# Cosine attention and a leaky-ReLU block on one core: norms issued 12 steps sooner in the visits, one remainder tile moved to a visit's end

## The chip, the cores and the metric

The kernel runs on 1 core of one Trainium2 chip. The metric is device time in microseconds (us): the median of the runs of one program. A profiled execution gives the trace; its span runs from the first to the last instruction, and its own device time lies a little above the span.

## The reference

Cosine attention over 8 batches, 12 heads, 448 tokens and head size 64, then two dense layers with a leaky ReLU between them:

```python
q_n = q / (norm(q) + 1e-06); k_n = k / (norm(k) + 1e-06)
scores = q_n @ k_n.T / tau
attn = exp(scores - max) / sum
x = (attn @ v), heads side by side        # 3584 x 768
h = x @ w_in                              # 768 x 2048
out = maximum(0.01 * h, h) @ w_out        # 2048 x 768
```

## The kernel before

**Tiles.** Two heads make a pair, called a slot `s` in the code: 6 slots in a batch, 48 in all. The 448 tokens of a head are 3 blocks of 128 (block `ki` = 0, 1, 2) and a remainder of 64. A *key tile* `(s, ki)` is the scores of one key block of a slot against all 448 queries, for both heads: two matmuls on TensorE (L259) into a pair of PSUM banks, and one exponential on ScalarE (L271) that reads the pair. The remainders of two slots together make one *remainder tile*, written `(s, 3)` with odd `s`: four matmuls that read the transposed queries and keys of slots `s - 1` and `s`, and again one exponential.

**A norm** of slot `s` (`norm`, L637) is a chain over five queues. `sums` (L178) are two VectorE reductions of squares that GpSimd made before (L167). `roots` are two ScalarE activations (L185, L186). `normalise` is four VectorE instructions (L197, L198, L202 twice) that write `qn`. `transposes` is a transposing DMA on SyncE's queue (L234) that turns `qn` into `qkT`, the operand of the key tiles. Then come the four loads of a later slot (`load_qk`, SyncE's queue), a one-element copy on GpSimd that waits for `qn` (`hold`, L478), and the squares of slot `s + 1` on GpSimd. So the squares of one slot start when the slot before it is normalised.

**The order of work.** The schedule is written by hand: each engine takes its instructions in the order in which the program issues them, and an instruction that waits holds all behind it on its engine or queue. Batches 3 to 7 each have a *visit* (the loop at L691). With `s0 = 6 * b`, a visit is:

1. `attend` for groups of four heads of the batch before: totals and products on TensorE (L282), reciprocal totals on ScalarE (L293, L294), scaling on VectorE (L313). Batch 3 has one of these here, the others three.
2. Loads of V on GpSimd's queue (L146, L154).
3. Two remainder tiles, `(s0 + 1, 3)` and `(s0 + 3, 3)` (L700).
4. *Tokens*: blocks of 128 output rows of an earlier chunk of the second dense layer (`both_halves`, L392). A token is 32 steps of two matmuls (L412) that gather in one pair of banks, kept for the whole token. Between the steps, by the table `after`, the 18 key tiles of the batch are issued. There are 3 tokens in the visits of batches 3, 4 and 6 (tiles after steps 5, 11, 16, 16, 21 and 27 of each) and 4 in those of 5 and 7. At the token's end VectorE copies the rows out (L421) and SyncE's queue stores them (L388).
5. The last remainder tile, `(s0 + 5, 3)` (L714).
6. `first`: 16 groups of the first dense layer (six matmuls L336 and one ScalarE activation L343 each).

**Banks.** `banks` deals the pair that was dealt longest ago among those not kept; a token keeps one of the four pairs, so the key tiles turn over in the other three.

**Norms inside a visit, before.** At the top of token `i` (`i` = 0, 1, 2) `sums(s0 + 4 + i)`; after step 16 of that token, behind its two tiles there, `norm(s0 + 4 + i)`. During `first`: sums of `s0 + 7`, `s0 + 8`, `s0 + 9` at `m` = 0, 5, 10 and their norms at `m` = 2, 7, 12. So in a visit of 3 tokens the tiles of slot `s0 + 5` begin at step 16 of token 2, one token after the step at which its norm is issued. Slot `s0 + 3` of batch 3, slot 21, is normalised in the last unit ahead of that visit (L662, L663, L674).

Of the kernel before, what the change touches and what calls it, by code (L numbers as in the profile page):

```python
# [16 lines left out]
def kernel(  # L17
# [61 lines left out]
    def banks(count, keep=None, which=None):  # L79
        lo, hi = (0, 8) if not deals["apart"] else (0, 4) if count == 2 else (4, 8)  # L80
        x = which if which is not None else min(
            (i for i in range(lo, hi, count) if not set(range(i, i + count)) & set(sum(kept.values(), []))),
            key=lambda i: max(age[i : i + count]),
        )
        deals["n"] += 1
        age[x : x + count] = [deals["n"]] * count
        if keep:
            kept[keep] = list(range(x, x + count))
        return ps[:, x] if count == 1 else ps[:, x : x + count]

    def given_back(keep):
        deals["n"] += 1
        for i in kept.pop(keep):
            age[i] = deals["n"]
# [63 lines left out]
    def squares(s, engs=(gp, gp)):  # L158
        if s >= NSLOT:
            return  # L160
        tiles = []
        for x, eng, name in zip(raw[s], engs, ("sq0", "sq1")):
            sq = sqp.tile(list(x.shape), F32, name=name)
            if eng is nc.scalar:
                nc.scalar.activation(sq, x, func=AF.Square)
            else:
                eng.tensor_tensor(sq, x, x, op=ALU.mult)  # L167
            tiles.append(sq)
        sqs[s] = tiles

    def sums(s, parts=(0, 1)):
        if s >= NSLOT:
            return
        if s not in ss:
            ss[s] = smp.tile([128, 14], F32, name="ss")
        for i in parts:
            o = ss[s][:, 0:8] if i == 0 else ss[s][:, 8:14]
            nc.vector.tensor_reduce(  # L178
                o.rearrange("p (h t) -> p h t", h=2), sqs[s][i], axis=AX.X, op=ALU.add
            )  # L180

    def roots(s):
        if s >= NSLOT:
            return
        nc.scalar.activation(ss[s], ss[s], func=AF.Ln, bias=tiny)  # L185
        nc.scalar.activation(ss[s], ss[s], func=AF.Exp, scale=0.5)  # L186
        if s < 2:
            nc.scalar.activation(ss[s], ss[s], func=AF.Identity, bias=eps)
# [3 lines left out]
    def normalise(s):  # L192
        if s >= NSLOT:
            return
        r = smp.tile([128, 14], F32, name="r")
        if s >= 2:
            nc.vector.tensor_scalar_add(ss[s], ss[s], 1e-6)  # L197
        nc.vector.reciprocal(r, ss[s])  # L198
        qn[s] = qnp.tile([128, 7, 2, D], BF16, name="qn")
        for x, lo, hi, r0 in ((raw[s][0], 0, 4, 0), (raw[s][1], 4, 7, 8)):  # L200
            nt = hi - lo
            nc.vector.tensor_tensor(  # L202
                qn[s][:, lo:hi],
                x.rearrange("p h t d -> p t h d"),
                r[:, r0 : r0 + 2 * nt].rearrange("p (h t) -> p t h", h=2)
                .unsqueeze(3).to_broadcast([128, nt, 2, D]),
                op=ALU.mult,
            )
# [19 lines left out]
    def transposes(s):  # L228
        if s >= NSLOT:
            return  # L230
        dst = qtp.tile([128, 7, 128], BF16, name="qkT")
        qkT[s] = dst.rearrange("p t c -> p (t c)")
        if s >= DMA_FROM:
            nc.sync.dma_start(  # L234
                out=dst, in_=qn[s].rearrange("p t h d -> p (t h d)"), transpose=True
            )
            return
        tp = transposed()
        one(tp, s, 0, 7)
        nc.vector.tensor_copy(out=dst, in_=tp)  # L240
# [6 lines left out]
    def key_tiles(which):  # L247

        tiles = []
        for s, ki in which:  # L250
            sc = banks(2)
            tiles.append(sc)
            for i in range(2 if ki == 3 else 1):
                x = qkT[s - 1 + i] if ki == 3 else qkT[s]
                for a in range(2):
                    rows = slice(64 * a, 64 * a + 64)
                    out = sc[64 * i : 64 * i + 64] if ki == 3 else sc
                    c0, c1 = (448, 512) if ki == 3 else (512 + 128 * ki, 640 + 128 * ki)
                    nc.tensor.matmul(  # L259
                        out=out[:, a, :S], lhsT=x[rows, c0:c1], rhs=x[rows, 0:S],  # L260
                        start=True, stop=True,
                    )
        for (s, ki), sc in zip(which, tiles):
            if ki == 3:
                pr[s // 2] = prp.tile([128, 2, S], BF16, name="pr")
                dst = pr[s // 2]
            else:
                if s not in pe:
                    pe[s] = pep.tile([128, 3, 2, S], BF16, name="pe")
                dst = pe[s][:, ki]  # L270
            nc.scalar.activation(out=dst, in_=sc[:, :, :S], func=AF.Exp, scale=inv_tau)  # L271
# [50 lines left out]
    def chunk_cols(c):  # L322
        return (0, MAIN) if c % 2 == 0 else (MAIN, 512)
# [3 lines left out]
    def first(c, m, kts=range(KT)):  # L327

        c0, n = chunk_cols(c)
        if c not in hT:  # L330
            hT[c] = htp.tile([128, MT, 512], BF16, name="hT")
        if (c, m) not in pms:
            pms[c, m] = banks(1)
        pm = pms[c, m]
        for kt in kts:
            nc.tensor.matmul(  # L336
                out=pm[:, :n],
                lhsT=w_in_sb[:, kt, m * 128 : (m + 1) * 128],
                rhs=xT[c // 2][:, kt, c0 : c0 + n],
                start=(kt == 0), stop=(kt == KT - 1),  # L340
            )
        if kts[-1] == KT - 1:
            nc.scalar.activation(  # L343
                out=hT[c][:, m, :n], in_=pms.pop((c, m))[:, :n], func=AF.Prelu, alpha=0.01
            )
            if (c, m, 0) in kept:
                given_back((c, m, 0))
# [79 lines left out]
    for c in range(B):  # L427
        c0, n = chunk_cols(c)
# [47 lines left out]
    def hold(x):  # L476
        seen = smp.tile([128, 1], F32, name="seen")
        gp.tensor_copy(out=seen, in_=x)  # L478
# [27 lines left out]
    for s in range(NPAIR):  # L506
        j = s // 2 - 1 if s >= 2 else None
        even = s % 2 == 0
        n = s + 2 if s + 2 <= NPAIR else None
# [52 lines left out]
    def attend(j):  # L562
        totals(j)
        po = banks(2)
        for e in range(2):
            products(j, e, po[:, e])
        for e in range(2):
            scale(j, e)
# [64 lines left out]
    def load_next(s):  # L633
        for n in (s + 2,) if s <= NPAIR + 6 else (s + 2, s + 3) if s == NPAIR + 7 else (s + 3,):
            load_qk(n)

    def norm(s):  # L637
        if s >= NSLOT:
            return
        roots(s)  # L640
        normalise(s)
        transposes(s)
        load_next(s)
        hold(qn[s][:, 6, 0, 0:1])
        squares(s + 1)
# [45 lines left out]
    for b in range(3, B):  # L691
        for j in range(b * NQ - 1 if b == 3 else (b - 1) * NQ, b * NQ):
            attend(j)
        for j in range(b * NQ, (b + 1) * NQ):
            if j not in vb:
                load_v(j)
        load_v_rem(b + 1)
        s0 = b * NPAIR
        tiles = [(s0 + p, ki) for p in range(NPAIR) for ki in range(3)]
        key_tiles([(s0 + 1, 3), (s0 + 3, 3)])  # L700
        for i, (c, ts) in enumerate(tokens):
            if i < 3:
                sums(s0 + 4 + i)
            if len(tokens) == 3:
                after = {5: 1, 11: 1, 16: 2, 21: 1, 27: 1}
            else:
                after = {8: 1, 16: 2, 21: 1, 27: 1} if i < 2 else {8: 1, 16: 2, 24: 1}
            for n, _ in enumerate(both_halves(c, ts), 1):
                for _ in range(after.get(n, 0)):
                    key_tiles([tiles.pop(0)])  # L710
                if n == 16 and i < 3:
                    norm(s0 + 4 + i)
        assert not tiles
        key_tiles([(s0 + 5, 3)])  # L714
        for m in range(MT):
            if m in (0, 5, 10):
                sums(s0 + 7 + m // 5)
            if m in (2, 7, 12):
                norm(s0 + 7 + m // 5)
            first(b - 1, m)  # L720
        tokens = [(b - 1, ts) for ts in range(chunk_cols(b - 1)[1] // 128)]
    for j in range((B - 1) * NQ, B * NQ):
        attend(j)
# [40 lines left out]
```

## Time and profile before

| what | value |
|---|---|
| runs | 427.1, 427.34, 428.75 us; median 427.34 |
| profiled execution | 429.06 us, its span 427.2 us |
| mean granted TensorE clock | 0.995 |
| busy, share of the span | TensorE 96%, ScalarE 61%, VectorE 46%, GpSimd 32% |

By stage, from the busy time of each engine in stretches of the span (us):

| stretch | what | length | TensorE busy | ScalarE busy |
|---|---|---|---|---|
| 122.0 to 150.4 | end of batch 2, batch 3's attend and tokens | 28.40 | 25.60 | 20.78 |
| 173.0 to 193.7 | batch 4's tokens (3) | 20.70 | 20.11 | 18.50 |
| 221.4 to 246.6 | batch 5's tokens (4) | 25.20 | 25.20 | 18.42 |
| 269.2 to 289.9 | batch 6's tokens (3) | 20.70 | 20.09 | 18.49 |
| 317.7 to 342.8 | batch 7's tokens (4) | 25.10 | 25.10 | 18.07 |

In the profile PE is TensorE's matmuls, PEld its weight loads, ACT ScalarE, DVE VectorE, POOL GpSimd, SP SyncE's queue. A line of a timeline gives the start, the length, engine, source line, operation, tiles and count of the instructions merged into it; in brackets stands the idle time before it and what ended that. PEclk is the granted TensorE clock as a share of full speed.

### The profile page before, as it was taken

To read this page: it belongs to the slowest core of one execution; us is meant where nothing else is said; L and a number is where in the kernel's file an instruction comes from. 1 tells how busy PE (TensorE), PEld (TensorE's weight loads), DVE (VectorE), ACT (ScalarE), POOL (GpSimd) and SP (SyncE) were. 2 spreads that over 40 slices of the span, in tenths; PEclk is the share of its full clock that TensorE was granted. 3 is DMA by queue.
4 is the path that set the end of the run, shared out by engine and by line. 5 is a ranking of instruction groups with operands and counts; after the bars stand their busy time and mean duration, and the time that the engine had idled before them with its cause. 6 is when DMAs were issued, how large, how long until landed. Compare 5 with 4: busy or idle time off the path is not lost.

```text
span 427.2 us, 9731 instructions
## 1 busy us (share of the span) xinstructions
PE 410.6 (96%) x3873; PEld 213.9 (50%) x3873; DVE 197.5 (46%) x412; ACT 262.6 (61%) x448; POOL 136.8 (32%) x208
## 2 busy tenths in 40 slices
PE   8689999999989999999999999999999999999995
PEld 3234455544435555554455555554455555554563
DVE  5785867646562564555444454555444201310021
ACT  3887785678856965885568665885568655114300
POOL 4757523543474235333351315333321000000000
PEclk9999999999998999999999999999999999999999
DMA  7999997997587787586384756576362410010022
GB/s 173 186 245 230 209 221 130 182 202 156 129 130 122 173 187 145 58 176 173 90 124 88 182 144 137 61 174 175 88 78 60 97 38 2 39 75 0 0 75 74
DMA packets 102894, 53.72 MB, mean 126 GB/s; under 512 B 68929, under 2 KB 97857, under 8 KB 102849
## 3 DMA queue, kind: packets, MB, share of 16 engines
q1 hardware_dynamic: 77296, 40.98, 40.2%
q0 software_dynamic: 25056, 11.80, 21.8%
q8 instruction: 30, 0.49, 0.5%
q10 hardware_dynamic: 496, 0.33, 0.2%
q14 instruction: 16, 0.12, 0.1%
HBM read 45.61 MB, written 11.01 MB: 133 GB/s over the span
## 4 chain that ended last, share of the span: by engine, by line
PE 87%; DMA 6%; DVE 3%; SPq 1%; issue 1%; ACT 1%; POOL 0%; POOLq 0%; DVEq 0%
PE ps L336 34%; PE ps L412 20%; PE ps L366 14%; PE ps L282 12%; PE ps L259 7%; DMA qkT<-qn 3%; DMA q_h<-in_q_dram 3%; DVE qn L202 2%; DMA q_h<-in_k_dram 1%; SPq L131 1%; PE ps L216 1%; ACT pe L271 0%; DVE ss L197 0%; DVE qkT L240 0%; DVE xT L313 0%
## 5 line engine op out<-in xcount | busy, mean ns | idle before, releaser
L336 PE MATMUL ps<-xT,w_in_sb 128*128 128x384 bf16 (+1 forms) x768 | 149.2, 353 | 0.9 <-DVE xT L313 0.9
L271 ACT ACTIVATE pe<-ps 128x896 bf16<-128x896 f32 x144 | 125.6, 914 | 28.9 <-PE ps L259 27.8
L343 ACT ACTIVATE hT<-ps 128x384 bf16<-128x384 f32 (+1 forms) x128 | 68.4, 542 | 71.2 <-PE ps L336 70.6
L336 PEld LDWEIGHTS <-w_in_sb 128*128 128x128 bf16 x768 | 73.8, 98 | 71.7 <-issue 5.1
L412 PE MATMUL ps<-w_out_sb,hT 64*128 64x384 bf16 x1088 | 102.6, 326 | 0.0
L412 PEld LDWEIGHTS <-hT 64*128 64x128 bf16 x1088 | 53.0, 95 | 39.5 <-issue 3.2
L178 DVE TENSOR_REDUCE ss<-sq 128x8 f32<-128x512 f32 (+1 forms) x96 | 58.2, 616 | 27.2 <-POOL sq L167 23.6
L478 POOL CAST seen<-qn 128x1 f32<-128x1 bf16 x47 | 8.6, 183 | 168.6 <-DVE qn L202 168.4
L259 PE MATMUL ps<-qkT 64*128 64x448 bf16 (+1 forms) x384 | 53.4, 358 | 7.6 <-DMA qkT<-qn 4.0
L366 PE MATMUL ps<-w_out_sb,hT 128*128 128x384 bf16 x352 | 58.9, 326 | 0.0
L313 DVE TENSOR_TENSOR xT<-ps,rb 128x448 bf16<-128x448 f32 x48 | 27.8, 619 | 49.3 <-ACT rb L294 49.3
L167 POOL TENSOR_TENSOR sq<-q_h 128x512 f32<-128x512 f32 x46 | 47.7, 1037 | 4.4 <-DMA q_h<-in_k_dram 3.6
L366 PEld LDWEIGHTS <-hT 128*128 128x128 bf16 x352 | 33.8, 98 | 24.0 <-issue 2.1
L197 DVE TENSOR_SCALAR ss<-ss 128x14 f32<-128x14 f32 x46 | 9.7, 212 | 73.1 <-ACT ss L186 73.0
L167 POOL TENSOR_TENSOR sq<-k_h 128x384 f32<-128x384 f32 x46 | 37.8, 822 | 0.0
L377 DVE COPY osb<-ps 128x384 f32<-128x384 f32 (+1 forms) x22 | 12.0, 547 | 51.7 <-PE ps L366 51.7
L282 PE MATMUL ps<-pe,v_b 128*32 128x448 bf16 x576 | 35.6, 353 | 0.0
L202 DVE TENSOR_TENSOR qn<-q_h,r 128x512 bf16<-128x512 f32 x48 | 33.5, 699 | 1.9 <-DMA q_h<-in_q_dram 0.3
L259 PEld LDWEIGHTS <-qkT 64*128 64x128 bf16 (+1 forms) x384 | 15.5, 97 | 33.2 <-issue 17.6
L271 ACT ACTIVATE pr<-ps 128x896 bf16<-128x896 f32 x24 | 21.6, 917 | 8.2 <-PE ps L259 8.2
L202 DVE TENSOR_TENSOR qn<-k_h,r 128x384 bf16<-128x384 f32 x48 | 26.5, 552 | 0.0
L293 ACT ACTIVATE rb<-ps 128x448 f32<-128x448 f32 x24 | 13.1, 544 | 19.4 <-PE ps L282 19.4
(43 smaller groups left out, 231.6 us busy)
## 6 DMA issues: line engine op xcount, KB each, us to landing
q_h<-in_q_dram SPq DMA_DIRECT2D x48, 192.0 KB, 3.1
k_h<-in_k_dram SPq DMA_DIRECT2D x47, 192.0 KB, 3.1
out_dram<-osb SPq DMA_DIRECT2D x30, 192.0 KB, 2.7
v_b<-in_v_dram POOLq DMA_DIRECT2D x24, 192.0 KB, 5.1
out_dram<-osb SPq DMA_DIRECT2D x12, 384.0 KB, 2.7
w_in_sb<-in_moe_w_in_dram POOLq DMA_DIRECT2D x4, 768.0 KB, 9.9
w_out_sb<-in_moe_w_out_dram POOLq DMA_DIRECT2D x2, 1536.0 KB, 17.5
q_h<-in_q_dram SPq DMA_DIRECT2D x48, 32.0 KB, 3.2
```

Of the source, the lines that this page charges most:

```text
L167: eng.tensor_tensor(sq, x, x, op=ALU.mult)
L178: nc.vector.tensor_reduce(o.rearrange("p (h t) -> p h t", h=2), sqs[s][i], axis=AX.X, op=ALU.add)
L202: nc.vector.tensor_tensor(qn[s][:, lo:hi], x.rearrange("p h t d -> p t h d"), r[:, r0 : r0 + 2 * nt].rearrange("p (h t) -> p t h", h=2) .u ...
L259: nc.tensor.matmul(out=out[:, a, :S], lhsT=x[rows, c0:c1], rhs=x[rows, 0:S], start=True, stop=True,)
L271: nc.scalar.activation(out=dst, in_=sc[:, :, :S], func=AF.Exp, scale=inv_tau)
L282: nc.tensor.matmul(out=x[32 * g : 32 * g + 32, :S], lhsT=weights(g, ki) if ki < 3 else rem(g), rhs=pe[s][:, ki, a, :] if ki < 3 else pr[j] ...
L293: nc.scalar.activation(rb, sm[:, :S], func=AF.Ln)
L313: nc.vector.tensor_tensor(xT[m][:, 2 * jj + e, half * S : (half + 1) * S], pos.pop((j, e))[:, :S], rbs[j], op=ALU.mult,)
L336: nc.tensor.matmul(out=pm[:, :n], lhsT=w_in_sb[:, kt, m * 128 : (m + 1) * 128], rhs=xT[c // 2][:, kt, c0 : c0 + n], start=(kt == 0), stop= ...
L343: nc.scalar.activation(out=hT[c][:, m, :n], in_=pms.pop((c, m))[:, :n], func=AF.Prelu, alpha=0.01)
L366: nc.tensor.matmul(out=po2[:, :HALF], lhsT=hT[c][:, m, ts * 128 : (ts + 1) * 128], rhs=w_out_sb[:, m, half * HALF : (half + 1) * HALF], st ...
L412: last[half] = nc.tensor.matmul(out=po2[:, half, :HALF], lhsT=hT[c][rows, m, ts * 128 : (ts + 1) * 128], rhs=w_out_sb[rows, m, half * HALF ...
```

## The change

The remainder tile `(s0 + 3, 3)` of batch 3's visit leaves the visit's start and is issued at its end, ahead of `(s0 + 5, 3)`; the other batches keep both at the start. The norm of slot `s0 + 4 + i` is issued after step 4 of token `i`, and so ahead of the token's first tile. The sums of `s0 + 5` and `s0 + 6` are issued after step 26 of tokens 0 and 1, and so ahead of the copy of these tokens' rows on VectorE. The sums of `s0 + 4` are issued at the end of the visit before, behind its last group of `first`, so that the next visit's attend with its scaling follows them on VectorE; batch 3 has no visit before it and issues them after its attend, ahead of token 0, as before. No instruction is added or removed: each engine has the same set, in another order.

```diff
-        key_tiles([(s0 + 1, 3), (s0 + 3, 3)])
+        key_tiles([(s0 + 1, 3), (s0 + 3, 3)][: 1 if b == 3 else 2])
+        if b == 3:
+            sums(s0 + 4)
         for i, (c, ts) in enumerate(tokens):
-            if i < 3:
-                sums(s0 + 4 + i)
...
             for n, _ in enumerate(both_halves(c, ts), 1):
                 for _ in range(after.get(n, 0)):
                     key_tiles([tiles.pop(0)])
-                if n == 16 and i < 3:
+                if n == 4 and i < 3:
                     norm(s0 + 4 + i)
+                if n == 26 and i < 2:
+                    sums(s0 + 5 + i)
         assert not tiles
-        key_tiles([(s0 + 5, 3)])
+        key_tiles([(s0 + 3, 3), (s0 + 5, 3)][0 if b == 3 else 1 :])
         for m in range(MT):
...
             first(b - 1, m)
+        sums(s0 + 10)
         tokens = [(b - 1, ts) for ts in range(chunk_cols(b - 1)[1] // 128)]
```

## Prediction

> **What bounds the kernel now.** I read the page's busy shares first, then the chain that ended last, then TensorE's waits.
>
> ```profile
> PE 410.6 (96%) x3873; PEld 213.9 (50%) x3873; DVE 197.5 (46%) x412; ACT 262.6 (61%) x448; POOL 136.8 (32%) x208
> ```
>
> TensorE is busy for all but 427.2 - 410.6 = 16.6 us. The chain gives PE 87% of the span, so a reordering can gain only where TensorE stands still. TensorE's waits over the whole span (engine and line, what it waited for, us in total, times, longest):
>
> ```profile
> PE ps L259 <- DMA qkT<-qn: 4.0, 4, 2.1
> PE ps L259 <- ACT pe L271: 2.3, 5, 1.1
> ```
>
> The second row falls before 50 us: asked from 50 us on, the waits show only the first. So behind the first batch TensorE is held by four transposing DMAs that land late, and by nothing else. TensorE's timeline places them:
>
> ```profile
> 125.40 0.57 PE L259 MATMUL ps<-qkT 64*64 64x448 bf16 x6
> 128.10 0.38 PE L259 MATMUL ps<-qkT 64*64 64x448 bf16 x2 [2.13 <-DMA qkT<-qn]
> ...
> 145.74 0.35 PE L259 MATMUL ps<-qkT 64*128 64x448 bf16 x2
> 146.76 0.36 PE L259 MATMUL ps<-qkT 64*128 64x448 bf16 x2 [0.66 <-DMA qkT<-qn]
> ...
> 190.08 0.36 PE L259 MATMUL ps<-qkT 64*128 64x448 bf16 x2 [0.59 <-DMA qkT<-qn]
> ...
> 286.30 0.36 PE L259 MATMUL ps<-qkT 64*128 64x448 bf16 x2 [0.61 <-DMA qkT<-qn]
> ```
>
> The first is batch 3's second remainder tile: half of it issues (the last two of the six matmuls), then slot 21's transposed tile is missing. The others are the first tile of slot s0 + 5, in token 2 of the three visits with 3 tokens; those with 4 tokens have no wait. Finally the stretches around the first wait (length, then busy us of PE, PEld, DVE, ACT, POOL with counts, then the granted clock, DMA share, GB/s):
>
> ```profile
> 125.97:128.10 2.13, 0.00 (x1) 0.00 (x2) 1.61 (x3) 0.78 (x1) 2.13 (x4) 1.00 1.01 149
> 128.10:129.00 0.90, 0.90 (x10) 0.51 (x12) 0.00 (x0) 0.48 (x1) 0.90 (x2) 1.00 0.88 237
> 129.00:132.25 3.25, 3.25 (x24) 1.55 (x21) 0.00 (x0) 1.35 (x2) 2.15 (x4) 0.51 1.31 176
> ```
>
> 0.9 us after the gap the granted clock is 0.51 for 3.25 us; the stretches that I read between 134.8 and 358.5 are at 1.00.
>
> **What the change is worth, step by step.**
>
> *The moved remainder tile.* A remainder tile takes 0.38 us, so the two would have ended at 125.40 + 0.76 = 126.16; the row says 128.10 + 0.38 = 128.48. Loss: 2.31 us (the idle time shows 2.13, as the last matmul's drain counts as busy). Token 0 needs only slots 18 and 19, so the wait goes and nothing takes its place there: (21, 3) now stands some 19 us later, and slot 21's DMA had landed at 128.1. Its 0.38 us on TensorE and 0.9 us on ACT are moved, not saved. Gain **2.31 us**.
>
> *The half clock.* From the first L412 to token 1's first tile is 128.41 to 137.24 = 8.83 us in batch 3, and 173.48 to 180.64 = 7.16 us in batch 4 with the same work. The slow clock cost 1.67 us. I take it as an answer to the gap: it is TensorE's longest after the first loads. Bounds: 0 if it has another cause, **1.67** if it goes. I take that for the profiled execution. The runs speak for it too: 427.1 and 427.34 against 428.75, and 429.06 profiled, steps of 1.4 to 2.0 us, as if two of four executions had the slow stretch.
>
> [...]
>
> *Slot s0 + 5's norm.* In token 2 the next tile follows 0.19 us behind the first one of step 16 where nothing waits (134.26 to 134.45 and the like). So the losses are 146.76 - 145.93 = 0.83, 190.08 - 189.33 = 0.75, 286.30 - 285.53 = 0.77. Now follow the chain in batch 4, whose visit start doesn't change. ACT, after the two remainder exponentials, reaches the roots at about 175.0 instead of 178.47; sums of s0 + 4 are long done. Roots to `qn` takes 178.47 to 180.70 = 2.2 us, so `qn` is there at 177.2. Then hold and squares 2.0 us (180.84 to 182.87) and the rest of the reductions 0.6 us (182.87 to 183.45): sums of s0 + 5 at about 179.9. Token 0 ends near 180.0, its copies (1.02 us) at 181.0. Roots of s0 + 5 follow the exponential of step 27, at 180.7, `qn` at 182.95, and the DMA lands 2.9 to 3.3 us later, near 186.0, instead of 190.08; wanted at 189.3. That is 3.3 us to spare for a wait of 0.75. The rows' store and the loads stand ahead of this transpose on SP's queue as before; the copy that the store waits for ends 2 us before `qn`. Even the longest landing of a transpose in this trace, 5.1 us, fits. The four loads behind each transpose go out as much sooner, into a buffer whose last readers (normalise and squares of the slot before) are done by then; the transpose itself writes slot s0's buffer (five are in turn), last read by (s0, 2) at step 16 of token 0. On GpSimd only the squares stand behind the hold. Gain **0.83 + 0.75 + 0.77 = 2.35 us**, bounds 0 and 2.35.
>
> *What the sooner norms put in ACT's way.* The roots (0.46 us net) stand ahead of the token's six exponentials, where before four ran first. Exponentials in a row start every 0.81 to 0.88 us: a token asks ACT for 6 x 0.84 + 0.46 = 5.5 us of its 6.33 (180.64 to 186.97). In batch 4 this makes step 5's exponential 0.46 us later, ending at 176.4; its pair is dealt again to the second tile of step 16 at 176.66. It fits by 0.26 us: nothing lost, 0.2 at worst.
>
> Batch 3's token 0 is the tight one, as its sums are not early:
>
> ```profile
> 126.42 1.34 DVE L178 TENSOR_REDUCE ss<-sq 128x8 f32<-128x512 f32 x2
> ...
> 128.67 2.48 POOL L154 DMA_DIRECT2D v_rem<-in_v_dram  x4
> ...
> 143.74 1.25 SPq L234 DMA_TRANSPOSE qkT<-qn  x1
> ```
>
> Token 0 now starts at 125.8. ACT ends the remainder's exponential at 126.75 and then waits in the roots for these sums until 127.8 (before, the roots came at 135.08). Behind it step 5's exponential runs 128.26 to 129.18, though its matmuls are done by 126.95. The second tile of step 16 wants that pair at 128.90 and starts at 129.23: **0.33 us lost**, bounds 0 and 1.0 (ACT's whole wait). From there ACT wins back 6.33 - 5.5 = 0.8 us a token.
>
> GpSimd delays the next norm: the V loads end at 131.15, so hold and squares of slot 23 run to 133.2, sums to 133.8, copies of token 0's rows to 134.8 (that pair is dealt again at 135.4), roots at 133.8, `qn` at 136.0. The transpose, 143.74 in the row above, is issued at 136.0 and lands near 139.0; wanted at 141.9. At the visit's end both remainder tiles find their pairs free: the exponentials of step 16's second tile and step 21 end at 143.8 and 144.7, the tiles come at 145.0 and 145.4. `first` begins near 145.8 instead of 150.4.
>
> *Visits with 4 tokens; sums of s0 + 10.* Nothing waits there now, and ACT has more room (18.4 of 25.2 us busy). The sums of s0 + 10 stand ahead of the attend's scaling: their squares end at 167.4, the sums at 168.0, the scaling starts at 168.23. Cost 0; without that 0.2 us the scaling slips, which TensorE doesn't wait for within the attends' 6.9 us.
>
> *Sum.* Against the profiled execution: 2.31 + 1.67 + 2.35 - 0.33 = 6.00; 429.06 - 6.00 = 423.06 us. Against the median, taken as a run without the slow stretch: 4.33; 427.34 - 4.33 = 423.01. Both give **423.0 us**.
>
> **Rivals.**
> 1. *All runs had the slow stretch, and it goes* (their spread is noise): 427.34 - 6.00 = 421.3. The first three times speak against it, being 1.4 us apart in two clusters.
> 2. *The half clock is no answer to the gap and stays*: against the profiled execution 429.06 - 4.33 = 424.7. [...]
> 3. *The norms come no sooner than the tiles need* (copies now behind the sums, the store ahead of the transpose): the 2.35 stays lost, 427.34 - 2.31 + 0.33 = 425.4, no change. The slack of 3.3 and 2.9 us speaks against it.
> 4. *Slower: ACT waits in each token's roots for the sums*, which now need the squares of the same token. Roots to the next sums is 2.2 + 2.0 + 0.6 = 4.8 us; batch 3's token 0 has 6.0 with GpSimd's V loads. It costs TensorE only if this loop exceeds the token's 6.33 us; then each token takes as long as the loop. Over the 9 tokens of the short visits it eats the gain at 6.8 us, and at 7.1 us the kernel is 2.4 us slower: 429.8. No row shows a loop so long outside of batch 3's start.
>
> **How the numbers follow.** 0.5% is 2.1 us, about what a measurement of this kernel can tell from no change. Forecast 0.62 (422.4 to 424.2), rival 1 0.15, rival 2 0.10, rival 3 0.07, rival 4 0.06. Faster by over 0.5% (below 425.2): the first three, 0.87, less 0.01 for their edge; same 0.08; slower 0.06. The range runs from rival 1 to rival 2: 421.2 to 424.9.
>
> **What would show it.** No TensorE wait for a transposing DMA after 100 us; granted clock 1.00 from 125 to 146; `first` of batch 3 near 145.8; a short wait of an L259 for ACT near 129; batch 4's and 6's tokens 0.75 us shorter, 5's and 7's unchanged. I am wrong if TensorE waits for L271 by more than 1 us in all, or the clock drops at another place.

## The result and the profile after

| | before | after |
|---|---|---|
| runs, us | 427.1, 427.34, 428.75, 429.42 | 422.4, 422.73, 423.05, 423.24 |
| median, us | 428.04 | 422.89 |
| profiled execution, us (span) | 429.06 (427.2) | 422.73 (420.9) |

The ratio is 0.9876, 95% interval 0.9843 to 0.9909: the changed kernel is 1.2% faster. In a later set it took 422.75 us (median of 6) against 427.27 (median of 17), ratio 0.989, interval 0.987 to 0.991. The forecast was 423.0.

The executions of before fall into two groups, with nothing between 427.35 and 428.38 us; the median depends on how many of each are in it. What divides them is the subject of the third experiment.

TensorE's line of the busy shares and the chain by engine, from the page of the changed kernel:

```profile
PE 408.0 (97%) x3873; PEld 214.9 (51%) x3873; DVE 197.9 (47%) x412; ACT 261.1 (62%) x448; POOL 137.1 (33%) x208
...
PE 87%; DVE 4%; DMA 3%; ACT 3%; issue 1%; SPq 1%; POOL 0%; POOLq 0%; ACTq 0%; DVEq 0%
```

TensorE's busy time fell by 2.6 us with the same instructions, mostly because matmuls at half clock count as busy for longer (twelve of L412 2.13 us in before, from 129.76, and 1.14 to 1.16 at the full clock). Its idle time fell from 16.6 to 12.9 us, and in the chain (the work that ended last, followed back) the DMAs' share from 6% to 3%. Asked for from 60 us on, TensorE's waits have no row left. Its timeline at batch 3's tokens:

```profile
125.29 0.38 PE L259 MATMUL ps<-qkT 64*64 64x448 bf16 x4
125.61 0.99 PE L412 MATMUL ps<-w_out_sb,hT 64*128 64x384 bf16 x10
...
128.60 0.86 PE L259 MATMUL ps<-qkT 64*128 64x448 bf16 x4
129.28 0.99 PE L412 MATMUL ps<-w_out_sb,hT 64*128 64x384 bf16 x10
...
141.57 0.56 PE L259 MATMUL ps<-qkT 64*128 64x448 bf16 x4
...
145.04 0.57 PE L259 MATMUL ps<-qkT 64*64 64x448 bf16 x8
145.54 2.77 PE L336 MATMUL ps<-xT,w_in_sb 128*128 128x384 bf16 x16
```

Token 0 starts 0.32 us behind the first remainder tile (before: 3.0 us). The two tiles of step 16 take 0.86 us in token 0 and 0.56 in token 2: that is the new stall of 0.3 us. In token 2 they now run together, where before the second came 0.83 us late. Both remainder tiles stand at the end (x8), and `first` begins at 145.54 instead of 150.35. The stretch that had half the clock, for the changed kernel (length, busy us of PE, PEld, DVE, ACT, POOL with counts, granted clock, DMA share, GB/s):

```profile
129.00:132.25 3.25, 3.15 (x38) 2.14 (x39) 1.06 (x2) 3.25 (x6) 3.25 (x7) 1.00 1.02 117
```

The clock is 1.00, and 38 matmuls stand where there were 24. ScalarE's timeline shows why the stall comes:

```profile
125.73 0.92 ACT L271 ACTIVATE pr<-ps 128x896 bf16<-128x896 f32 x1 [0.67 <-PE ps L259]
127.69 0.31 ACT L185 ACTIVATE ss<-ss,tiny 128x14 f32<-128x14 f32 x1 [1.04 <-DVE ss L178]
128.03 0.21 ACT L186 ACTIVATE ss<-ss 128x14 f32<-128x14 f32 x1
128.15 4.94 ACT L271 ACTIVATE pe<-ps 128x896 bf16<-128x896 f32 x6
```

It waits 1.04 us in the roots for VectorE's sums, then runs six exponentials without a break; the first of them, whose matmuls end at 126.43 + 0.35 = 126.78, could have started near 126.8.

### The profile page after: what moved, and what is told of

Read it like the earlier page. It is cut to its first block, busy times and chain, and to the rows that moved or that the text cites. A ratio compares the mean times of both kernels' runs of the same rounds, so it can differ in the third digit from the quotient of the medians.

```text
span 420.9 us, 9733 instructions
## 1 busy us (share of the span) xinstructions
PE 408.0 (97%) x3873; PEld 214.9 (51%) x3873; DVE 197.9 (47%) x412; ACT 261.1 (62%) x448; POOL 137.1 (33%) x208
## 4 chain that ended last, share of the span: by engine, by line
PE 87%; DVE 4%; DMA 3%; ACT 3%; issue 1%; SPq 1%; POOL 0%; POOLq 0%; ACTq 0%; DVEq 0%
PE ps L336 34%; PE ps L412 20%; PE ps L366 13%; PE ps L282 12%; PE ps L259 7%; DMA q_h<-in_k_dram 3%; DVE qn L202 2%; ACT pe L271 1%; DVE ss L178 1%; PE ps L216 1%; SPq L131 0%; ACT ss L185 0%; ACT ss L186 0%; DVE r L198 0%; DVE xT L313 0%
## 5 line engine op out<-in xcount | busy, mean ns | idle before, releaser
L271 ACT ACTIVATE pe<-ps 128x896 bf16<-128x896 f32 x144 | 122.9, 919 | 25.1 <-PE ps L259 24.5
L412 PE MATMUL ps<-w_out_sb,hT 64*128 64x384 bf16 x1088 | 101.4, 323 | 0.0
L412 PEld LDWEIGHTS <-hT 64*128 64x128 bf16 x1088 | 53.8, 94 | 37.5 <-issue 1.6
L259 PE MATMUL ps<-qkT 64*128 64x448 bf16 (+1 forms) x384 | 52.4, 355 | 3.7 <-ACT pe L271 2.3
L421 DVE COPY osb<-ps 128x384 f32<-128x384 f32 x34 | 17.4, 552 | 35.9 <-PE ps L412 25.9
```

Of the source, the lines that this page charges most:

```text
L259: nc.tensor.matmul(out=out[:, a, :S], lhsT=x[rows, c0:c1], rhs=x[rows, 0:S], start=True, stop=True,)
L412: last[half] = nc.tensor.matmul(out=po2[:, half, :HALF], lhsT=hT[c][rows, m, ts * 128 : (ts + 1) * 128], rhs=w_out_sb[rows, m, half * HALF ...
L421: nc.vector.tensor_copy(out=o[:, half * HALF : (half + 1) * HALF], in_=po2[:, half, :HALF])
```

## The experiments

**1. The remainder tile alone.** Before, with only the first and the last key tiles of the change:

```diff
-        key_tiles([(s0 + 1, 3), (s0 + 3, 3)])
+        key_tiles([(s0 + 1, 3), (s0 + 3, 3)][: 1 if b == 3 else 2])
...
-        key_tiles([(s0 + 5, 3)])
+        key_tiles([(s0 + 3, 3), (s0 + 5, 3)][0 if b == 3 else 1 :])
```

> Only the remainder tile (s0+3,3) of batch 3 is moved to the visit's end; norms and sums stay as before. My theory (the gap costs its own length, and the half clock answers to it): the 2.1 us wait near 128 is gone, the granted clock is 1.00 from 125 to 146, the three waits of 0.6 to 0.7 us for the transposed slot s0+5 stay. Against an execution of before with the slow stretch the span falls by 2.5 + 1.7 = 4.2 us, against one without it by 2.5 us: some 424 to 425.5 us. Rival (the half clock has another cause): a stretch at about 0.5 of some 3 us stays near 129 to 132, and the time is 2.5 us under before in every execution.

424.63 us (5 runs, 424.26 to 425.09); ratio to before 0.9933, interval 0.9909 to 0.9957. Against the lower group of before on this chip (9 of 14 executions, median 426.86) that is 2.2 us less, against the upper (5, median 428.6) 4.0 us. TensorE's waits from 60 us on:

```profile
PE ps L259 <- DMA qkT<-qn: 2.0, 3, 0.8
```

The long wait is gone, the three short ones are left, and the granted clock is 1.00 in every stretch read from 118 to 146. None of the five executions lies in an upper group. As my theory expected, 0.3 us short.

**2. The norms alone.** The changed kernel with both remainder tiles back in their old places (the two lines of experiment 1 undone).

> Only the norms and sums are moved; batch 3's second remainder tile stays at the visit's start. My theory: the wait of 2.1 us near 128 stays and with it a stretch at half clock in those executions that have one before; the three waits of 0.6 to 0.7 us are gone: 2.35 us under before, some 425.4 us. The 0.3 us stall of batch 3's token 0 does not come, as ACT has the time of the gap for the roots. Rival (the norms come no sooner than the tiles need): the three waits stay and the time is that of before within 0.5 us.

424.47 us (4 runs, 423.64 to 424.81); ratio 0.9925, interval 0.9899 to 0.9951; 2.4 us under the lower group. One wait is left, that of the remainder tile, and no stall follows it in token 0:

```profile
127.47 0.38 PE L259 MATMUL ps<-qkT 64*64 64x448 bf16 x2 [1.88 <-DMA qkT<-qn]
```

So the two parts are worth nearly the same and add up: 2.2 + 2.4 = 4.6 us apart, 4.35 us together (422.75 against 427.10, the lower group on the chip of experiments 5 to 8), the 0.3 us stall coming in only when both are made. On the clock it says little: the profiled execution had this gap of 1.88 us and its clock stayed at 1.00, and four executions are too few to say that the upper group, some two in five of before, is gone.

**3. The gap filled.** Before, with useless matmuls where TensorE waited; the extra results are overwritten by the tile.

```diff
             tiles.append(sc)
+            for _ in range(pad if tiles[1:] else 0):
+                nc.tensor.matmul(out=sc[:, 0, :S], lhsT=warm[:, :128], rhs=warm[:, :S], start=True, stop=True)
...
-        key_tiles([(s0 + 1, 3), (s0 + 3, 3)])
+        key_tiles([(s0 + 1, 3), (s0 + 3, 3)], 11 if b == 3 else 0)
```

> Before, with 11 matmuls of no use (448 columns, about 0.19 us each, written into the pair that the second remainder tile then overwrites) between batch 3's two remainder tiles, so that TensorE works through the time in which it waited. My theory: the tile still comes at about 128.1 to 128.5, but the granted clock stays at 1.00 and token 0 takes 6.4 us: the span is 1.7 us under that of an execution of before with the slow stretch, and no execution is near 429. Rival (the half clock comes from something else at that place, such as the V loads): the clock falls to 0.5 near 129 as before and the span is that of before.

426.98 us, all 10 executions between 426.84 and 427.46; ratio to all of before 0.9991, interval 0.9975 to 1.0007. TensorE's timeline and the stretch after it:

```profile
125.35 2.25 PE L254 MATMUL ps<-warm 128*128 128x448 bf16 x11
127.53 0.38 PE L263 MATMUL ps<-qkT 64*64 64x448 bf16 x4
127.85 0.99 PE L416 MATMUL ps<-w_out_sb,hT 64*128 64x384 bf16 x10
```

```profile
129.00:132.25 3.25, 3.25 (x44) 1.88 (x40) 0.00 (x0) 2.85 (x4) 1.80 (x3) 1.00 1.22 157
```

The tile comes nearly as late as in before (token 0 starts 127.85 - 125.03 = 2.82 us behind the first tile, in before 3.01), yet the clock stays at 1.00, and the ten times are those of the lower group alone (426.86). The V loads run at the same place (GpSimd busy, 157 GB/s). So here it is the idle time that brings the half clock, not what else happens at that place. That the upper group of before is the executions that have it, and the lower one those without, is an inference: the only trace of before is of the upper group. It fits the size, as the groups are 1.74 us apart on this chip and 1.75 on that of experiments 5 to 8, and the slow stretch cost 1.67. The mean granted clock of an execution doesn't divide them: where it is on record it is 0.994 or 0.995 in the upper group, but 0.994 to 1.000 in the lower one and with the gap filled; in experiment 6 the fastest of ten executions, 425.78 us, has 0.996, and four from 426.19 to 426.51 us have 1.000. Over all runs, 16 of 37 executions of before lie in the upper group; of the 47 executions of kernels without this gap none lies so far above the others of its kernel.

**4. Gaps made on purpose.** The changed kernel with VectorE reductions of no use, and a TensorE instruction that waits for the last of them ahead of token 0 of batches 4 to 7:

```diff
+    idle_in = cpool.tile([128, 512], F32, name="idle_in")
+    nc.vector.memset(idle_in, 1.0)
+    idle_out = cpool.tile([128, 8], F32, name="idle_out")
...
+        for n in range({4: 1, 5: 2, 6: 3, 7: 4}.get(b, 0)):
+            idle = nc.vector.tensor_reduce(
+                idle_out, idle_in.rearrange("p (h d) -> p h d", d=D), axis=AX.X, op=ALU.add
+            )
+        if b > 3:
+            tc.add_manual_dep(nc.tensor.nop().ins, idle.ins.name, ...)
```

> The changed kernel with one artificial gap on TensorE ahead of token 0 of batches 4, 5, 6 and 7: it waits there for 1, 2, 3 and 4 VectorE reductions of no use (0.65 us each, behind the attend's scaling), so gaps of about 0.9, 1.6, 2.2 and 2.9 us. My theory: the gaps near 2.2 and 2.9 us are each followed within some 3 us by a stretch of about 3.3 us at half clock, the one of 0.9 us is not, the one of 1.6 us is open; each slow stretch adds about 1.6 us to its gap. [...]

The gaps were 1.03, 1.75, 2.47 and 3.19 us, and only the third brought a slow stretch: the longest didn't, and behind the first two the clock is 1.00 too (169.52 to 172.92, 219.00 to 222.40). The last two gaps, and the granted clock behind them (the slow stretch begins already inside the third gap, near 268.6, with 0.82 between 268 and 269, and ends before the stretch shown does):

```profile
269.10 1.78 PE L412 MATMUL ps<-w_out_sb,hT 64*128 64x384 bf16 x10 [2.47 <-DVE idle_out L707]
321.47 1.47 PE L412 MATMUL ps<-w_out_sb,hT 64*128 64x384 bf16 x16 [3.19 <-DVE idle_out L707]
```

```profile
269.20:272.60 3.40, 3.40 (x26) 1.66 (x27) 1.96 (x4) 0.92 (x1) 1.85 (x3) 0.58 0.39 54
321.67:325.07 3.40, 3.40 (x44) 2.01 (x42) 1.95 (x4) 1.32 (x2) 1.95 (x3) 1.00 0.28 57
```

My theory fell in the part that a longer gap does it more surely. That no gap does it is out as well. One execution, 432.4 us. Two more kernels then asked whether chance, place or size decides. Four equal gaps (`{4: 3, 5: 3, 6: 3, 7: 3}`):

> The changed kernel with four artificial gaps of the same size, 3 VectorE reductions of no use ahead of token 0 of batches 4, 5, 6 and 7 (2.47 us measured for that count). Theory A (a gap of 2 to 3 us halves the clock by chance, as it falls against something that runs by itself; 15 of 36 executions of before lie in the upper cluster): some of the four are followed by a slow stretch of about 3 us and some are not. Theory B (the place decides: batch 6's visit): only the gap of batch 6 is followed by one. Theory C (the size decides, 2.5 us does it and 3.2 us does not): all four are.

and the four sizes in the other order (`{4: 4, 5: 3, 6: 2, 7: 1}`):

> The changed kernel with the four gaps in the other order: 4, 3, 2 and 1 reductions ahead of token 0 of batches 4, 5, 6 and 7, so gaps of about 3.2, 2.5, 1.75 and 1.0 us. Theory A: the 1.0 us gap is followed by no slow stretch, the longer ones by chance. Theory B: the one of batch 6, here 1.75 us, is. Theory C: that of 2.5 us in batch 5 is and that of 3.2 us in batch 4 is not.

One execution of each, 436.96 and 435.68 us. The stretches behind the four equal gaps of 2.47 us, batches 4 to 7:

```profile
172.41:175.81 3.40, 3.40 (x44) 1.97 (x42) 1.95 (x4) 2.05 (x3) 1.95 (x3) 1.00 0.41 61
222.62:226.02 3.40, 3.40 (x44) 2.01 (x42) 1.95 (x4) 1.32 (x2) 1.95 (x3) 1.00 0.42 65
272.92:276.32 3.40, 3.40 (x24) 1.64 (x22) 1.94 (x4) 0.92 (x1) 1.96 (x3) 0.50 0.40 60
324.12:327.52 3.40, 2.91 (x20) 1.33 (x22) 1.92 (x6) 0.05 (x1) 1.26 (x3) 0.50 0.06 14
```

Two of four equal gaps halve the clock, two don't. In the other order:

```profile
173.50:176.90 3.40, 3.40 (x26) 1.62 (x22) 1.89 (x4) 1.06 (x2) 2.00 (x3) 0.50 0.35 68
224.70:228.10 3.40, 3.35 (x22) 1.58 (x24) 1.92 (x5) 0.17 (x1) 1.71 (x3) 0.50 0.42 55
276.15:279.55 3.40, 3.40 (x44) 1.99 (x42) 1.81 (x5) 2.13 (x4) 1.79 (x4) 1.00 0.41 40
324.92:328.32 3.40, 3.40 (x44) 2.02 (x42) 1.58 (x4) 2.09 (x5) 0.76 (x2) 1.00 0.02 5
```

Here 3.19 us in batch 4 and 2.47 us in batch 5 do it; 1.75 and 1.03 don't. Place is out (each of the four batches has had one, and none has one always), and so is size alone; batch 5 has had a gap of 2.47 us twice, once with a slow stretch and once without. Over the three kernels: 0 of 2 at 1.0 us, 0 of 2 at 1.75, 4 of 6 at 2.47, 1 of 2 at 3.19. Theory A is left in its first part, chance; what a gap falls against, if anything, no run shows.

**5. The changed kernel again, beside the next three.**

> The changed kernel beside the next three. If the two parts add up (2.2 us for the tile alone, 2.4 for the norms alone, less the 0.3 us stall that needs both) it lies 4.3 us under those executions of before that have no slow stretch (about 426.9 on the chip of the runs before), so some 422.5 us, and no execution lies 1.7 us above the others.

422.75 us (6 executions, 422.29 to 423.32), 4.35 us under the lower group of before on this chip (10 of 17, median 427.10); 4.3 was expected.

**6. The sums behind the copies.** The changed kernel with the sums of s0 + 5 and s0 + 6 at the top of the tokens:

```diff
+            if 0 < i < 3:
+                sums(s0 + 4 + i)
...
-                if n == 26 and i < 2:
-                    sums(s0 + 5 + i)
```

> The changed kernel, but the sums of s0+5 and s0+6 stand at the top of tokens 1 and 2 as before, behind the copies of the rows, with the norms at step 4. My theory: ScalarE then waits in the roots for copies and sums; in the visits with 3 tokens the exponential of step 5 ends some 0.7 us after its pair is wanted by the second tile of step 16, in tokens 1 and 2: 6 stalls of L259 for L271 of about 0.7 us, 4.3 us over the changed kernel, so about the time of before; in those with 4 tokens none. Rival (the place of the sums does not matter, as no engine has work for the whole token): the time of the changed kernel within 0.5 us.

426.27 us (10 runs); ratio to before 0.9966, interval 0.9951 to 0.9982. That is 3.5 us over the changed kernel. The waits from 60 us on (TensorE's), and ScalarE's timeline in batch 4:

```profile
PE ps L259 <- ACT pe L271: 2.3, 6, 0.4
PE ps L336 <- ACT pe L271: 0.2, 1, 0.2
```

```profile
171.44 4.94 ACT L271 ACTIVATE pe<-ps 128x896 bf16<-128x896 f32 x6
178.10 0.31 ACT L185 ACTIVATE ss<-ss,tiny 128x14 f32<-128x14 f32 x1 [1.72 <-DVE ss L178]
178.44 0.22 ACT L186 ACTIVATE ss<-ss 128x14 f32<-128x14 f32 x1
178.56 4.94 ACT L271 ACTIVATE pe<-ps 128x896 bf16<-128x896 f32 x6
```

Six stalls in the places expected, none in the visits with 4 tokens. Each costs 179.51 - 178.96 = 0.55 us (the row says 0.39, counted from 178.77 + 0.35 = 179.12, the end of the matmuls before); I had said 0.7. With the wait of 0.2 us at the end of batch 3's visit they make 6 x 0.55 + 0.2 = 3.5 us, the whole difference. An engine that is 61% busy over the span of before gives 3.5 of the 4.35 us back, because it is asked to wait 1.50 to 1.72 us ahead of six exponentials.

**7. The first norm later.** The changed kernel with batch 3's first norm behind step 11:

```diff
-                if n == 4 and i < 3:
+                if n == (11 if b == 3 and i == 0 else 4) and i < 3:
```

> The changed kernel, but in token 0 of batch 3 the norm is issued behind step 11's tile instead of step 4, so that two exponentials run while ScalarE would wait for the sums. My theory: the stall of 0.3 us at the second tile of step 16 goes, nothing else moves (GpSimd is held by the V loads until 131 anyway): 0.3 us under the changed kernel. Rival (the norm has to be that early): slot 22's or 23's transposed tile comes late and TensorE waits for a DMA near 139 or 142.

422.51 us (6 runs, 422.08 to 422.8), 0.24 under the changed kernel: the runs' spreads overlap, so the time doesn't settle it. The stage does: from the first remainder tile to `first` is 124.86 to 144.92 = 20.06 us, in the two traces of the changed kernel 20.25 and 20.29. The stall of 0.3 us is gone from token 0, a smaller one of 0.12 us comes in token 1 (its two tiles of step 16 take 135.00 - 134.50 = 0.50 us instead of 0.38), and no DMA is waited for.

**8. Four steps instead of twelve.** Experiment 1 with the norms at step 12, all sums as before:

```diff
-                if n == 16 and i < 3:
+                if n == 12 and i < 3:
```

> Before with the moved remainder tile and the norms at step 12 instead of 16, so ahead of the two tiles there; all sums stay at the top of the tokens. My theory: the two exponentials that the norm overtakes give 1.4 us, more than the waits of 0.75 to 0.83 us, the sums are done by then, and ScalarE is not held: no wait for a DMA, no stall in batch 3's token 0, 0.3 us under the changed kernel. Rival (12 steps were needed): waits for the transposed slot s0+5 of some tenths of a us are left.

422.62 us (6 runs, 421.64 to 422.8), 0.13 under the changed kernel, no wait of TensorE from 60 us on, the stage 20.00 us. So four steps are enough, with no sums moved, and the rival falls. Experiments 7 and 8 and the changed kernel can't be told apart by time here; by the stage the two are 0.2 to 0.3 us ahead.

## Why the prediction was right

It was right in the time, in the mechanism and in nearly every term. By its steps:

- *The moved remainder tile*, 2.31 predicted (2.32 by its own rows). Token 0 started 3.01 us behind the first tile's start, now 0.32: 2.69. The tile costs 0.18 at the visit's end (0.50 for both tiles there against 0.32 for one). So 2.51 us. The step that was off is the price of a tile: the row's 0.38 us runs 0.06 us past the start of the next matmuls (125.29 + 0.38 = 125.67 against 125.61). Nothing took the wait's place.
- *The half clock*, 1.67. The profiled execution of before had it, the changed kernel hasn't. That the lower times of before are executions without it was inferred from three runs; experiment 3 supports it. The gap alone doesn't bring the half clock, as the prediction took it: 16 of 37 executions have it, and that the profiled one was among them was chance. Rival 1 (all runs had it) and rival 2 (it stays) are out. It is why one forecast came out of two starting points, 429.06 - 6.00 and 427.34 - 4.33.
- *The three waits for slot s0 + 5*, 0.83 + 0.75 + 0.77. The tokens of batches 4 and 6, from the chain in order of time, went from 20.19 (173.55 to 193.74) and 20.20 to 19.42 (168.75 to 188.17) and 19.42 us; batch 5's, with 4 tokens, stayed at 24.6. Batch 3's stage shortened by 150.35 - 125.40 - 20.25 = 4.70 = 2.51 + 1.67 + 0.83 - 0.32. Rival 3 is out.
- *The stall*, 0.33. The two tiles take 0.86 instead of 0.54 us: 0.32.
- *SyncE's queue* was reckoned too quick. Slot 23's transpose was to be issued at 136.0:

```profile
134.22 1.15 SPq L131 DMA_DIRECT2D q_h<-in_k_dram  x1
135.48 2.04 SPq L388 DMA_DIRECT2D out_dram<-osb  x2
137.62 1.29 SPq L234 DMA_TRANSPOSE qkT<-qn  x1
```

The load and the store ahead of it, 0.65 and 1.19 us in before, took 1.15 and 2.04, and the transpose landed 3.6 us after its issue, near 141.2, not 3.0. The tile that needs it was due at 141.57 + 0.19 = 141.76. So of the 2.9 us to spare about 0.5 were left. It cost nothing, but it was the thinnest part of the argument.
- *Sums of s0 + 10*, 0: the scaling follows them by 0.3 us (163.08, 163.42) and waits for ScalarE, not for them.
- *Rival 4* (each token waits for the sums in ScalarE) didn't come: behind token 0's 1.04 us the wait is 0.55 us in batch 3's token 1, where TensorE doesn't feel it, and nothing in batch 4. Experiment 6 shows that its mechanism is real: with the sums behind the copies 3.5 of the 4.35 us are gone. (By the rival's own numbers its 7.1 us for 9 tokens give 429.9, not 429.8.)

Against the profiled execution the sum was 6.00; the time fell by 429.06 - 422.73 = 6.33: 0.2 from the tile, and the tokens of batch 3 begin 0.11 us sooner for no reason in the change.

## What to carry to other kernels

Where one engine is busy 96% of the time, list its few waits, place each, and ask only how much sooner the operand must come: here 0.8 us, for which four steps do as well as twelve. A chain moved ahead in program order past its inputs must have these moved too, or the engine that carries it stands waiting in front of work that was ready (experiment 6: 3.5 of 4.35 us). And compare executions by groups before comparing medians, when one gap can cost 1.7 us more in one execution and not in the next.

## What the hardware showed that I had not expected

A gap of 2.1 to 3.2 us on TensorE halves its granted clock for 3.40 to 3.42 us, or doesn't: behind four equal gaps of 2.47 us in one execution it is 1.00, 1.00, 0.50 and 0.50. The lengths are worked out from the clock in slices of 1 us, in before and the three kernels of experiment 4. In before the slow stretch runs from 129.06 (0.53 between 129 and 130) to 132.48 (0.76 between 132 and 133).

Of the gaps looked at, the shortest with a slow stretch behind it is 2.13 us, in the profiled execution of before (0.51 over 3.25 us). The longest without one is 3.19 us (1.00 over 3.40 us). Behind 1.88 us in experiment 2 and 1.75 us in two kernels of experiment 4 the clock stayed at 1.00. Of the eight gaps of 2.47 and 3.19 us five were followed by the half clock, and by the groups of times 16 of 37 executions of before (43%) had it.

So the length of a gap alone doesn't tell whether it costs the 1.67 us, and neither does its place. What does, these runs don't show.
